# One decode step of attention beside an MLP: the rounds of the loops and the joining of the partial softmaxes rewritten

## Chip, core and metric

The kernel runs on one core of a Trainium2 chip. The metric is the device time of one execution in microseconds. Three runs of the kernel before gave 675.93, 675.94 and 676.19 us; their median is 675.94.

## What is computed

Two tokens (B = 2) go through two branches, which a gate mixes. Branch A is a multi-head attention with a cache: 16 heads of width 256, 4096 cached keys and values per head and token, all float32. Branch B is an MLP with 1792 hidden columns.

```python
g = sigmoid((x * gate_w).sum(-1, keepdims=True))
q = (x @ wq).reshape(B, Sq, H, Dh).transpose(0, 2, 1, 3)      # x: 2 x 1 x 448
scores = einsum("bhqd,bhkd->bhqk", q, k_cache) * Dh ** -0.5
o = einsum("bhqk,bhkd->bhqd", softmax(scores), v_cache)
a = o.transpose(0, 2, 1, 3).reshape(B, Sq, H * Dh) @ wo       # 4096 x 448
b = maximum(einsum("bsd,df->bsf", x, w1), 0) @ w2
return g * a + (1 - g) * b
```

The caches hold 268 MB, which are read once.

## The kernel before

A **unit** is one head of one token; there are U = 32. Its keys and values, 64 KB for each of 128 partitions (8.39 MB), come with one DMA into one of three slots of SBUF. SP issues all large loads, in this order: `wq` into slot 2, units 0 and 1 into slots 0 and 1, the other units in a loop of ten rounds of three (`more`, L126), then `w12` in two halves into slot 2 (`w1`, `w2`) and `wo` into slot 0 in eight pieces (`late`, L135; the limits of the pieces are `CUTS`, in chunks of 448 columns, 32 in all). Ahead of each load SP waits for the slot's own semaphore (`free`), which VectorE raises after the last operation on a unit; the first one TensorE raises, when `wq` has been used.

Per unit, three engines take turns, tied by the semaphores query, score, top, prob and room. ScalarE copies the unit's query out of `qt` (`pick`, L248, one of three buffers), TensorE multiplies it with the keys into the PSUM tile `ps` (`scores`, L234), VectorE takes the negated maximum `nm` of each row, ScalarE the exponential `prob` with its row sums `ls` (`softmax`, L252), and VectorE eight multiplications with the values in place, whose row sums are the partial outputs `ov` (`values`, L259). TensorE may begin the next unit once the first of the eight is done. The keys of a unit are dealt to four groups of 32 partitions, so each unit has four partial softmaxes.

Each of the three engines has a loop of ten rounds with three units written out in a round (L275). Units 30 and 31 stand behind the loop, written out.

**Joining** (`combine`, L285) makes one softmax of the four partial ones, for 16 units at a time: transposes of `nm` and `ls`, a minimum, exponentials, a sum, a reciprocal and the weights `wb` with the gate; a product with the identity that spreads them over the partitions; their product with `ov` (`os`); four products with `sel` that add up the partitions; and copies into `ot`, which is the stationary operand for `wo`. The first half is joined between units 29 and 30. The second half is joined behind the MLP's second layer, and between its steps TensorE multiplies the first eight chunks of `wo`.

The MLP's layers stand behind unit 31 on TensorE: the first waits for `w1`, the second (14 chunks, `acc`) for `w2`.

**The end** (`project`, L364): chunks 0 to 23 of `wo` are added up in `acc` in four column groups. VectorE copies `acc` to SBUF, and TensorE folds the four groups into `z` with `fold`. The last eight chunks (`TAIL`) are multiplied straight into `z`, in four products each. One copy to `res` and a store end the kernel. Float32 products are issued as two instructions each, so a chunk in `acc` is two instructions and a direct chunk is eight.

Of the kernel before, what the change touches and what calls it, by code (L numbers as in the profile page):

```python
# [8 lines left out]
P, HP = 128, 64  # L9
# [58 lines left out]
def gated_mix_decode(nc, xg, kv, wq, w12, wo, out):  # L68
# [15 lines left out]
    UB = U // NB  # L84
# [4 lines left out]
    assert U == LOOPS * SLOTS + 2 and SLOTS == 3  # L89
# [4 lines left out]
    def bank(name, n=CW):  # L94
# [4 lines left out]
    TAIL = 8  # L99
    names = [*ENGINES, "xg", "w2", *(f"wo{k}" for k in CUTS[1:]), "query", "score", "top", "prob", "room",  # L100
             *(f"land{s}" for s in range(SLOTS)), *(f"free{s}" for s in range(SLOTS)), "out"]
    sem = {n: nc.alloc_semaphore(n) for n in names}
    land = [sem[f"land{s}"] for s in range(SLOTS)]
    free = [sem[f"free{s}"] for s in range(SLOTS)]
# [5 lines left out]
    slot = [sbuf(f"slot{s}", P, LEN) for s in range(SLOTS)]  # L110
# [24 lines left out]
    def late(e):  # L135
        take(e, free[2])
        load(2, w12, land[2], 0, NF * D)(e)
        load(2, w12, sem["w2"], NF * D)(e)
        take(e, free[0])
        for lo, hi in zip(CUTS, CUTS[1:]):  # L140
            load(0, wo, sem[f"wo{hi}"], lo * D, hi * D)(e)
        take(e, free[1])
# [21 lines left out]
    xr = sbuf("xr", P, KC, G, B, RB)  # L164
    pr.raw(dve, lambda e: e.wait_ge(sem["xg"], 16))
    for g in range(G):
        pr.op(dve, lambda e, g=g: e.tensor_copy(xr[:, :, g], xg_sb[:, :, :B, None].to_broadcast([P, KC, B, RB])))  # L167
    xu = sbuf("xu", P, KC, UB // B, B)
    have_x = pr.op(dve, lambda e: e.tensor_copy(xu, xg_sb[:, :, None, :B].to_broadcast([P, KC, UB // B, B])))  # L169
# [16 lines left out]

    pr.raw(pe, lambda e: e.wait_ge(sem["xg"], 16))
    for c in range(KC):
        r = rows_of(c)
        t = mm(pw[0][:, :1], xr[r, c].rearrange("p g b r -> p (g b r)"), xg_sb[r, c, B:], c == 0, c == KC - 1, have_x)  # L190
    gp = sbuf("gp", P, 1)
    gate_read = t = activate(gp, pw[0][:, :1], AF.Sigmoid, t)
    omg = sbuf("omg", P, 1)
    have_omg = pr.op(dve, lambda e: e.tensor_scalar(omg, gp, -1.0, 1.0, op0=ALU.mult, op1=ALU.add), t)
    for c in range(KC):
        r = rows_of(c)
        t = mm(pw[1][:UB, :1], xu[r, c].rearrange("p u b -> p (u b)"), xg_sb[r, c, B:], c == 0, c == KC - 1)
    gu = sbuf("gu", UB, 1)
    have_gu = activate(gu, pw[1][:UB, :1], AF.Sigmoid, t)
# [8 lines left out]
    for i in range(NB):  # L208
        w = slot[2][:, i * WQ:(i + 1) * WQ]
        for c in range(KC):  # L210
            for g in range(G):
                r = rows_of(c, g // 2)
                at = g * W + c * CW if c < KF else G * W + g % 2 * CW
                lhs, rhs = flat(xr[r, c, g]), w[r, at:at + CW]
                last = mm(pw[2 + i][g * R:(g + 1) * R, :], lhs, rhs, c == 0, c == KC - 1)
        t = activate(wide, pw[2 + i], AF.Copy, last, *busy[1], scale=SCALE)
        pt = pw[i]
        for k in range(2 * T):
            t2 = transpose(pt[:, k * P:(k + 1) * P], wide[:, k * P:(k + 1) * P], t, gate_read, have_gu)
        busy[1] = (t2,)  # L220
        for s in range(2):
            dst = qt.rearrange("p t (i g s b) -> p i s t g b", i=NB, g=G, s=2)[:, i, s]
            src = pt[:, ::RB].rearrange("p (s t g b) -> p s t g b", s=2, t=T, g=G)[:, s]
            have_q = activate(dst, src, AF.Copy, t2)
# [7 lines left out]
    query = [sbuf(f"query{s}", P, T) for s in range(SLOTS)]  # L232

    def scores(e, u, s):  # L234
        take(e, land[s], 16)
        take(e, sem["query"])
        take(e, sem["room"])
        for c in range(SG // CW):
            for t in range(T):
                for g in range(G):  # L240
                    lo = t * S + g * SG + c * CW
                    m = e.matmul(ps[g * R:(g + 1) * R, c * CW:(c + 1) * CW],  # L242
                                 query[s][:, t:t + 1].to_broadcast([P, R]), slot[s][:, lo:lo + CW],
                                 start=(t == 0), stop=(t == T - 1))
                    if c == SG // CW - 1 and t == T - 1:
                        m.then_inc(sem["score"], 1)

    def pick(e, u, s):  # L248
        e.activation(query[s], qt[:, :, bass.ds(u, 1)].rearrange("p t o -> p (t o)"), AF.Copy).then_inc(  # L249
            sem["query"], 1)  # L250

    def softmax(e, u, s, more=True):  # L252
# [3 lines left out]
        if more:  # L256
            pick(e, u + 1, (s + 1) % SLOTS)

    def values(e, u, s):  # L259
# [3 lines left out]
        for j in range(J):  # L263
            v = slot[s][:, T * S + j * SG:T * S + (j + 1) * SG]
# [3 lines left out]
            if j == J - 1:  # L268
                m.then_inc(free[s], 1)

    stages = {pe: scores, act: softmax, dve: values}
    pr.raw(pe, lambda e: (e.sem_inc(sem["room"], 1), e.drain().then_inc(free[2], 1)))
    pr.raw(act, lambda e: pick(e, 0, 0), have_q)
    for e in stages:
        pr.loop(e, LOOPS, lambda e_, i, e=e: [stages[e](e_, i * SLOTS + s, s) for s in range(SLOTS)])  # L275

    nb, e4, el, lsum, rl = (sbuf(n, UB, k) for n, k in (("nb", 1), ("e4", G), ("el", G), ("lsum", 1), ("rl", 1)))
    wb = sbuf("wb", UB, G, R)  # L280
    os = sbuf("os", P, UB, J)
    ot = sbuf("ot", P, NB, HH, J, B, RB)


    def combine(i, done):  # L285
        us = slice(i * UB, (i + 1) * UB)
        tp, wp, po = pw[0], pw[1], pw[2]
        transpose(tp[:UB, :P], nm[:, us], done)
        t = transpose(tp[:UB, P:2 * P], ls[:, us])
        mt = tp[:UB, 0:P:R]  # L290
        lt = tp[:UB, P:2 * P:R]
        t = pr.op(dve, lambda e: e.tensor_reduce(nb, mt, axis=AX.X, op=ALU.min), t)  # L292
        t = activate(e4, mt, AF.Exp, t, bias=nb, scale=-1.0)
        t = pr.op(dve, lambda e: e.scalar_tensor_tensor(el, e4, 1.0, lt, op0=ALU.mult, op1=ALU.mult, accum_out=lsum),
                  t)
        t = pr.op(dve, lambda e: e.reciprocal(rl, lsum), t)
        t = pr.op(dve, lambda e: e.tensor_scalar(wb, e4[:, :, None].to_broadcast([UB, G, R]), rl, gu, op0=ALU.mult,
                                                 op1=ALU.mult), t, have_gu)
        yield
        t = mm(wp[:, :UB], wb.rearrange("u g r -> u (g r)"), ident[:UB, :UB], True, True, t)  # L300
        t = pr.op(dve, lambda e: e.tensor_tensor(os, ov[:, us], wp[:, :UB, None].to_broadcast([P, UB, J]),
                                                 op=ALU.mult), t)
        yield
        n = HH * B * J
        for q in range(G):
            t2 = mm(po[q * R:(q + 1) * R, :n], sel, os.rearrange("p u j -> p (u j)")[:, q * n:(q + 1) * n], True, True,
                    t)
        for hh in range(HH):
            t = pr.op(dve, lambda e, hh=hh: e.tensor_copy(  # L309
                ot[:, i, hh], po[:, hh * B * J:(hh + 1) * B * J].rearrange("p (b j o) -> p j b o", j=J, o=1)  # L310
                .to_broadcast([P, J, B, RB])), t2)
        have_ot.append(t)

    have_ot = []
    for _ in combine(0, pr.op(dve, lambda e: e.drain())):  # L315
        pass
    for u in range(LOOPS * SLOTS, U):
        for e, f in stages.items():
            more = (u + 1 < U,) if e == act else ()
            pr.raw(e, lambda e_, f=f, u=u, more=more: f(e_, u, u % SLOTS, *more))  # L320
# [9 lines left out]
    for c in range(KC):  # L330
        for g in range(G):
# [3 lines left out]
            t = mm(ph[g * R:(g + 1) * R, :FG], flat(xr[r, c, g]), w1[r, at:at + FG], c == 0, c == KC - 1)  # L335
    t = activate(hs, ph[:, :FG], AF.Relu, t, have_omg, *busy[1], scale=omg)
    for k in range(KF):
        t2 = transpose(pt[:, k * P:(k + 1) * P], hs[:, k * P:(k + 1) * P], t, have_ot[0])
# [9 lines left out]

    pr.raw(pe, lambda e: e.wait_ge(sem["w2"], 16))
    for k in range(NF):  # L350
        g = k % G
        mm(acc[g * R:(g + 1) * R, :], hr[:, k, :], w2[:, k * D:(k + 1) * D], k < G, False, have_hr)
    pr.raw(pe, lambda e: take(e, sem["room"]))
    w = slot[0]

    def lhs(k):
        i, k = divmod(k, HH * J)
        return flat(ot[:, i, k // J, k % J])

# [4 lines left out]
    def project(lo, hi):  # L364
        for k in range(lo, hi):
            if k in CUTS:
                pr.raw(pe, lambda e, s=sem[f"wo{CUTS[CUTS.index(k) + 1]}"]: e.wait_ge(s, 16))
            if k < n:
                g = k % G
                t = mm(acc[g * R:(g + 1) * R, :], lhs(k), w[:, k * D:(k + 1) * D], False, k >= n - G,  # L370
                       have_ot[k // (HH * J)])
            else:
                for g in range(G):
                    t = mm(z[g * R:(g + 1) * R, :DG], lhs(k), w[:, k * D + g * DG:k * D + (g + 1) * DG], False,
                           k == NO - 1)
# [79 lines left out]
```

## Time and profile before

| | |
|---|---|
| median of three runs | 675.94 us |
| profiled execution, its own time | 675.89 us |
| its span (first to last instruction) | 674.6 us |
| busy: VectorE, TensorE, ScalarE | 341.5, 220.4, 59.7 us |
| read from HBM | 289.54 MB, 429 GB/s over the span |

The span is what the trace shows; all times of rows count from its start. Busy times add up the instructions of an engine. TensorE's are modelled and overlap each other, since matmuls are pipelined. For a kernel of this kind the rate of the DMA over the span and what happens after the last landing tell more than the busy shares.

### The profile page before, as it was taken

What the parts mean: (1) busy time and instruction counts of PE and PEld (TensorE: products, weight loads), DVE (VectorE), ACT (ScalarE), POOL (GpSimd) and SP (SyncE); (2) the same over time, 40 slices, a digit from 0 to 9 for tenths busy, and PEclk for the clock granted to TensorE, in tenths of its full rate; (3) what the DMA queues carried; (4) which work ended last, traced back from release to release, by engine and by line L of the source; (5) the groups of instructions that cost most, each with busy time, mean ns of one, the idle gap of its engine ahead of it and who ended that gap; (6) DMA issues with size and microseconds to landing.
All of it is one profiled execution on the core that took longest, in us unless ns stands there. A gap on an engine that the chain in (4) does not pass through costs nothing. (4 is left out here: it accounts for less than half of the span.)

```text
span 674.6 us, 4162 instructions
## 1 busy us (share of the span) xinstructions
PE 220.4 (33%) x1323; PEld 67.6 (10%) x1323; DVE 341.5 (51%) x571; ACT 59.7 (9%) x121; POOL 0.7 (0%) x6
## 2 busy tenths in 40 slices
PE   0653212333332213333321233333223333331367
PEld 0210000001001000100100010010001001000012
DVE  0006565643655665364566636455564643657661
ACT  0010001001000100100010010001001001000010
POOL 0000000000000000000000000000000000000000
PEclk9976566776656677676556667655666766655789
DMA  9999999999999999999999999999999999999997
GB/s 381 428 435 436 436 435 435 435 435 435 435 435 435 435 435 435 435 435 435 431 435 435 435 435 435 435 435 435 435 435 435 431 435 435 435 435 435 403 424 310
DMA packets 6372, 289.61 MB, mean 429 GB/s; under 512 B 864, under 2 KB 1120, under 8 KB 1632
## 3 DMA queue, kind: packets, MB, share of 16 engines
q1 hardware_dynamic: 6224, 289.55, 99.3%
q8 instruction: 3, 0.05, 0.0%
q10 hardware_dynamic: 144, 0.01, 0.0%
q14 instruction: 1, 0.01, 0.0%
HBM read 289.54 MB, written 0.01 MB: 429 GB/s over the span
## 5 line engine op out<-in xcount | busy, mean ns | idle before, releaser
L265 DVE SCALAR_TENSOR_TENSOR slot<-slot,prob 128x1024 f32<-128x1024 f32 x256 | 295.9, 1221 | 65.3 <-DVEq L65 65.3
L242 PE MATMUL ps<-slot,query 128*32 128x512 f32 x1024 | 186.3, 890 | 406.4 <-PEq L65 406.3
L261 DVE TENSOR_REDUCE nm<-ps 128x1024 f32 (+1 forms) x32 | 39.2, 1224 | 228.8 <-DVEq L65 228.8
L242 PEld LDWEIGHTS ps<-slot,query 128*32 128x32 f32 x1024 | 55.7, 156 | 535.5 <-issue 534.9
L254 ACT ACTIVATE prob<-ps,nm 128x1024 f32<-128x1024 f32 x32 | 35.6, 1113 | 367.2 <-ACTq L65 367.1
L254 ACT ACT_TABLE_LOAD x10 | 12.8, 1283 | 178.7 <-ACTq L65 178.7
L265 DVE DVE_READ_ACCUMULATOR slot<-slot,prob (+1 forms) x256 | 21.2, 83 | 0.0
L178 PE MATMUL pw<-slot,xr 128*32 128x512 f32 (+3 forms) x96 | 13.5, 696 | 1.7 <-PEq L65 1.7
L167 DVE COPY xr<-xg_sb 128x128 f32<-128x128 f32 x4 | 0.6, 220 | 18.5 <-DMA xg_sb<-in_xg 18.5
L178 PE MATMUL pw<-xg_sb,xr 128*128 128x1 f32 (+1 forms) x8 | 1.9, 352 | 21.7 <-DVE xu L169 21.7
L178 PE MATMUL acc<-slot,hr 128*32 128x448 f32 x28 | 6.1, 945 | 2.7 <-DMA slot<-in_w 2.7
L249 ACT ACTIVATE query<-qt 128x2 f32 (+1 forms) x32 | 6.2, 193 | 0.0
L254 ACT ACTIVATION_READ_ACCUMULATOR prob<-ps,nm (+1 forms) x32 | 6.2, 193 | 0.0
L178 PE MATMUL acc<-slot,ot 128*32 128x448 f32 x48 | 5.4, 547 | 1.3 <-DMA slot<-in_wo 1.3
L181 PE MATMUL pw<-ident,nm 128*16 128x128 f32 x2 | 0.7, 330 | 12.6 <-DVEq L315 12.6
L178 PEld LDWEIGHTS pw<-slot,xr 128*32 128x32 f32 (+1 forms) x96 | 2.9, 122 | 10.7 <-issue 10.7
L178 PEld LDWEIGHTS pw<-xg_sb,xr 128*128 128x128 f32 (+1 forms) x8 | 1.8, 320 | 21.6 <-DMA xg_sb<-in_xg 21.6
L181 PE MATMUL pw<-ident,wide 128*128 128x128 f32 x11 | 1.9, 288 | 2.4 <-ACT wide L184 2.4
L383 DVE COPY wide<-acc 128x448 f32<-128x448 f32 x1 | 0.6, 625 | 3.9 <-PE acc L178 3.9
L292 DVE TENSOR_REDUCE nb<-pw 16x1 f32<-16x4 f32 x2 | 0.3, 150 | 4.5 <-PE pw L181 4.5
L178 PE MATMUL pw<-slot,ot 128*32 128x112 f32 x64 | 2.3, 265 | 0.3 <-DMA slot<-in_wo 0.2
L309 DVE COPY ot<-pw 128x256 f32<-128x256 f32 x4 | 1.5, 419 | 1.4 <-PE pw L178 1.4
(42 smaller groups left out, 20.3 us busy)
## 6 DMA issues: line engine op xcount, KB each, us to landing
slot<-in_wq SPq DMA_DIRECT2D x1, 7168.0 KB, 19.8
slot<-in_w SPq DMA_DIRECT2D x2, 3136.0 KB, 30.8
slot<-in_wo SPq DMA_DIRECT2D x2, 1792.0 KB, 20.3
slot<-in_wo SPq DMA_DIRECT2D x3, 896.0 KB, 25.6
slot<-in_kv SPq DMA_DIRECT2D x32, 39.0
slot<-in_wo SPq DMA_DIRECT2D x1, 448.0 KB, 27.9
slot<-in_wo SPq DMA_DIRECT2D x2, 224.0 KB, 28.0
xg_sb<-in_xg ACTq DMA_DIRECT2D x1, 6.0 KB, 20.0
```

Source lines behind the costliest of these rows:

```text
L167: pr.op(dve, lambda e, g=g: e.tensor_copy(xr[:, :, g], xg_sb[:, :, :B, None].to_broadcast([P, KC, B, RB])))
L178: return pr.op(pe, lambda e: e.matmul(out, lhs, rhs, start=start, stop=stop), *after)
L181: return pr.op(pe, lambda e: e.transpose(out, src, ident), *after)
L242: m = e.matmul(ps[g * R:(g + 1) * R, c * CW:(c + 1) * CW], query[s][:, t:t + 1].to_broadcast([P, R]), slot[s][:, lo:lo + CW], start=(t == ...
L249: e.activation(query[s], qt[:, :, bass.ds(u, 1)].rearrange("p t o -> p (t o)"), AF.Copy).then_inc(sem["query"], 1)
L254: e.activation(prob, ps, AF.Exp, bias=nm[:, bass.ds(u, 1)], accum_out=ls[:, bass.ds(u, 1)]).then_inc(sem["prob"], 1)
L261: e.tensor_reduce(nm[:, bass.ds(u, 1)], ps, axis=AX.X, op=ALU.max, negate=True).then_inc(sem["top"], 1)
L265: m = e.scalar_tensor_tensor(v, v, 1.0, prob, op0=ALU.mult, op1=ALU.mult, accum_out=ov[:, bass.ds(u, 1), j])
L292: t = pr.op(dve, lambda e: e.tensor_reduce(nb, mt, axis=AX.X, op=ALU.min), t)
L309: t = pr.op(dve, lambda e, hh=hh: e.tensor_copy(ot[:, i, hh], po[:, hh * B * J:(hh + 1) * B * J].rearrange("p (b j o) -> p j b o", j=J, o= ...
L383: t = pr.op(dve, lambda e: e.tensor_copy(a_sb, acc), t)
```

## The change

- TensorE runs eleven rounds of the loop over all units: two units, and behind a condition on the round a third one, which the last round leaves out. ScalarE and VectorE run 32 rounds of one unit each. Nothing is written out behind the loops.
- VectorE finds a unit's slot by arithmetic on a register; the three slots are one tensor. The query has one buffer, which ScalarE writes at the start of a round. The three `free` semaphores are one.
- All 32 units are joined at once. TensorE does the transposes behind the sixth of the 14 chunks of the MLP's second layer, the product with the identity behind the tenth, and the rest behind the fourteenth. No chunk of `wo` is multiplied before `ot` is there.
- `TAIL` is 4 for 8: chunks 24 to 27 go into `acc`.
- The stationary operands made of x hold one copy for a group, not four; a copy on ScalarE (`xw`) makes the wide one for the gate, and the gate for the 16 units of a half is no longer computed by itself.
- On the host, units are ordered by token first, then head.

The core of the diff:

```diff
-    TAIL = 8
+    TAIL = 4
@@ SP
-            take(e, free[s])
+            take(e, sem["free"])
@@ the units
+    def score_rounds(e, i):
+        for s in range(U - LOOPS * SLOTS):
+            scores(e, s)
+        with e.If(i < LOOPS):
+            for s in range(U - LOOPS * SLOTS, SLOTS):
+                scores(e, s)
+
-    def softmax(e, u, s, more=True):
+    def softmax(e, u):
+        e.activation(query, qt[:, :, bass.ds(u, 1)].rearrange("p t o -> p (t o)"), AF.Copy).then_inc(sem["query"], 1)
         take(e, sem["top"])
         e.activation(prob, ps, AF.Exp, bias=nm[:, bass.ds(u, 1)], accum_out=ls[:, bass.ds(u, 1)]).then_inc(
             sem["prob"], 1)
-        if more:
-            pick(e, u + 1, (s + 1) % SLOTS)
-    def values(e, u, s):
+    def values(e, u):
+        at = e.snap(u % SLOTS * LEN)
...
-            v = slot[s][:, T * S + j * SG:T * S + (j + 1) * SG]
+            v = slots[:, bass.ds(at + (T * S + j * SG), SG)]
...
+    pr.loop(pe, LOOPS + 1, score_rounds)
+    pr.loop(act, U, softmax)
+    pr.loop(dve, U, values)
@@ behind the loops
-    for _ in combine(0, pr.op(dve, lambda e: e.drain())):
-        pass
-    for u in range(LOOPS * SLOTS, U):
-        ...
+    second(0, NF - 8)
+    transpose(tp[:U, :P], nm, done)
+    t = transpose(tp[:U, P:2 * P], ls)
+    second(NF - 8, NF - 4)
...
+    t1 = mm(wp[:, :U], wb.rearrange("u g r -> u (g r)"), ident[:U, :U], True, True, t)
+    second(NF - 4, NF)
...
+    for q in range(G):
+        t2 = mm(po[q * R:(q + 1) * R, :NB * cols], sel, os[:, :, q].rearrange("p i h j b -> p i (h j b)"), True, True, t)
+    for i in range(NB):
+        have_ot.append(pr.op(dve, lambda e, i=i: e.tensor_copy(
...
-    at = 0
-    for _ in combine(1, done):
-        project(at, at + NO // 8)
-        at += NO // 8
-    t = project(at, n)
+    t = project(0, n)
```

## Rows read from the trace of the kernel before

**Rows 1.** The page's DMA rate in GB/s, in 40 equal slices of 16.9 us.
```profile
GB/s 381 428 435 436 436 435 435 435 435 435 435 435 435 435 435 435 435 435 435 431 435 435 435 435 435 435 435 435 435 435 435 431 435 435 435 435 435 403 424 310
```

**Rows 2.** The chain of waits that ended last, its end: start, length (us), what.
```profile
643.93 27.99 DMA slot<-in_wo
...
671.96 0.52 PE pw L178 x8
...
672.51 0.28 DVE res L388
```

**Rows 3.** The timeline, units 1 and 27: start, length (us), engine, line, operation [idle before <-releaser].
```profile
59.81 5.35 PE L242 MATMUL ps<-slot,query 128*32 128x512 f32 x32 [12.94 <-PEq L65]
...
562.59 6.61 PE L242 MATMUL ps<-slot,query 128*32 128x512 f32 x32 [13.36 <-PEq L65]
...
570.91 1.28 ACT L254 ACT_TABLE_LOAD   x1 [18.59 <-ACTq L65]
572.20 1.11 ACT L254 ACTIVATE prob<-ps,nm 128x1024 f32<-128x1024 f32 x1
```

**Rows 4.** The timeline, units 30 and 31 and the MLP.
```profile
628.66 1.23 DVE L261 TENSOR_REDUCE nm<-ps 128x1 f32<-128x1024 f32 x1 [4.75 <-DVEq L65]
...
639.87 5.45 PE L242 MATMUL ps<-slot,query 128*32 128x512 f32 x32 [11.46 <-PEq L65]
...
647.03 3.35 PE L178 MATMUL pw<-slot,xr 128*32 128x448 f32 x32 [1.71 <-PEq L65]
...
654.84 6.06 PE L178 MATMUL acc<-slot,hr 128*32 128x448 f32 x28 [2.71 <-DMA slot<-in_w]
...
656.30 1.22 DVE L265 SCALAR_TENSOR_TENSOR slot<-slot,prob 128x1024 f32<-128x1024 f32 x1
```

**Rows 5.** Sequencer instructions of single lines: count, shortest/median/longest ns, first to last start.
```profile
L46 PEldq COMPARE_BRANCH  x10: 76/208/217, 81.6 to 603.1; - x10
...
L254 ACT ACT_TABLE_LOAD  x10: 1283/1283/1283, 48.7 to 570.9; - x10
...
L265 DVEq FUSED_REGOPS  x240: 57/57/57, 51.3 to 611.7; - x120
```

**Rows 6.** The timeline, the joining of the first half.
```profile
620.00 0.42 PE L181 MATMUL pw<-ident,ls 128*16 128x128 f32 x1
...
621.70 0.60 PE L178 MATMUL pw<-ident,wb 16*128 16x16 f32 x2 [1.27 <-DVE wb L297]
622.34 0.29 DVE L301 TENSOR_TENSOR os<-ov,pw 128x128 f32<-128x128 f32 x1 [0.70 <-PE pw L178]
...
622.68 0.34 PE L178 MATMUL pw<-os,sel 128*32 128x32 f32 x8 [0.38 <-DVE os L301]
...
623.16 0.76 DVE L309 COPY ot<-pw 128x256 f32<-128x256 f32 x2 [0.54 <-PE pw L178]
```

**Rows 7.** The timeline, `wo` and the fold.
```profile
663.65 1.69 PE L178 MATMUL acc<-slot,ot 128*32 128x448 f32 x16
...
667.63 0.96 PE L178 MATMUL acc<-slot,ot 128*32 128x448 f32 x8 [1.17 <-DMA slot<-in_wo]
668.73 0.62 DVE L383 COPY wide<-acc 128x448 f32<-128x448 f32 x1 [3.89 <-PE acc L178]
...
669.41 0.40 PE L178 MATMUL pw<-wide,fold 128*32 128x112 f32 x8 [0.82 <-DVE wide L383]
669.78 0.73 PEld L178 LDWEIGHTS pw<-slot,ot 128*32 128x32 f32 x32 [0.22 <-DMA slot<-in_wo]
669.78 2.02 PE L178 MATMUL pw<-slot,ot 128*32 128x112 f32 x56
```

**Rows 8.** Busy time of each engine by stretch, then TensorE's granted clock, DMA share, GB/s.
```profile
660.00:662.00 2.00, 2.00 (x14) 0.26 (x10) 0.39 (x4) 0.25 (x1) 0.00 (x0) 0.84 0.95 405
```

**Rows 9.** The page: the queue for code (packets, MB, share), and `xg` (us to landing).
```profile
q8 instruction: 3, 0.05, 0.0%
...
xg_sb<-in_xg ACTq DMA_DIRECT2D x1, 6.0 KB, 20.0
```

More of the change, by code (lines that the diff above doesn't have):

```diff
@@ L88, in gated_mix_decode @@
     LOOPS = (U - 2) // SLOTS
-    assert U == LOOPS * SLOTS + 2 and SLOTS == 3
+    assert U == LOOPS * SLOTS + 2 and SLOTS == 3 and U == R
     def sbuf(name, *shape):
@@ L98, in gated_mix_decode @@
     CUTS = (0, NO // 4, NO // 2, NO - 12, NO - 8, NO - 4, NO - 2, NO - 1, NO)
-    TAIL = 8
-    names = [*ENGINES, "xg", "w2", *(f"wo{k}" for k in CUTS[1:]), "query", "score", "top", "prob", "room",
-             *(f"land{s}" for s in range(SLOTS)), *(f"free{s}" for s in range(SLOTS)), "out"]
+    TAIL = 4
+    names = [*ENGINES, "xg", "w2", *(f"wo{k}" for k in CUTS[1:]), "query", "score", "top", "prob", "room", "free",
+             *(f"land{s}" for s in range(SLOTS)), "out"]
     sem = {n: nc.alloc_semaphore(n) for n in names}
     land = [sem[f"land{s}"] for s in range(SLOTS)]
-    free = [sem[f"free{s}"] for s in range(SLOTS)]
     pr = Program(nc)
@@ L109, in gated_mix_decode @@
     sbuf("gap", P, -(-(-nc.sbuf_base // 32) * 32) % 1024 // 4)
-    slot = [sbuf(f"slot{s}", P, LEN) for s in range(SLOTS)]
+    slots = sbuf("slots", P, SLOTS * LEN)
+    slot = [slots[:, s * LEN:(s + 1) * LEN] for s in range(SLOTS)]
     ps = bank("ps", SG)
@@ L135, in late @@
     def late(e):
-        take(e, free[2])
+        take(e, sem["free"])
         load(2, w12, land[2], 0, NF * D)(e)
         load(2, w12, sem["w2"], NF * D)(e)
-        take(e, free[0])
+        take(e, sem["free"])
         for lo, hi in zip(CUTS, CUTS[1:]):
             load(0, wo, sem[f"wo{hi}"], lo * D, hi * D)(e)
-        take(e, free[1])
+        take(e, sem["free"])
     pr.raw(sp, late)
@@ L161, in gated_mix_decode @@
                                                      op0=ALU.mult), t)
-    xr = sbuf("xr", P, KC, G, B, RB)
+    xr = sbuf("xr", P, KC, B, RB)
     pr.raw(dve, lambda e: e.wait_ge(sem["xg"], 16))
[L166 to L169, printed above, removed]
+    have_x = pr.op(dve, lambda e: e.tensor_copy(xr, xg_sb[:, :, :B, None].to_broadcast([P, KC, B, RB])))
     def rows_of(c, i=0):
@@ L189, in gated_mix_decode @@
         r = rows_of(c)
-        t = mm(pw[0][:, :1], xr[r, c].rearrange("p g b r -> p (g b r)"), xg_sb[r, c, B:], c == 0, c == KC - 1, have_x)
+        t = mm(pw[0][:, :1], xw[r, c].rearrange("p g r -> p (g r)"), xg_sb[r, c, B:], c == 0, c == KC - 1, have_xw)
     gp = sbuf("gp", P, 1)
-    gate_read = t = activate(gp, pw[0][:, :1], AF.Sigmoid, t)
+    have_gp = gate_read = t = activate(gp, pw[0][:, :1], AF.Sigmoid, t)
     omg = sbuf("omg", P, 1)
     have_omg = pr.op(dve, lambda e: e.tensor_scalar(omg, gp, -1.0, 1.0, op0=ALU.mult, op1=ALU.add), t)
[L195 to L199, printed above, removed]
     qt = sbuf("qt", P, T, U)
@@ L218, in gated_mix_decode @@
         for k in range(2 * T):
-            t2 = transpose(pt[:, k * P:(k + 1) * P], wide[:, k * P:(k + 1) * P], t, gate_read, have_gu)
+            t2 = transpose(pt[:, k * P:(k + 1) * P], wide[:, k * P:(k + 1) * P], t, gate_read)
         busy[1] = (t2,)
         for s in range(2):
-            dst = qt.rearrange("p t (i g s b) -> p i s t g b", i=NB, g=G, s=2)[:, i, s]
+            dst = qt.rearrange("p t (b i g s) -> p i s t g b", i=NB, g=G, s=2)[:, i, s]
             src = pt[:, ::RB].rearrange("p (s t g b) -> p s t g b", s=2, t=T, g=G)[:, s]
@@ L231, in gated_mix_decode, with scores @@
     prob = sbuf("prob", P, SG)
-    query = [sbuf(f"query{s}", P, T) for s in range(SLOTS)]
-    def scores(e, u, s):
+    query = sbuf("query", P, T)
+    def scores(e, s):
         take(e, land[s], 16)
@@ L242, in scores @@
                     m = e.matmul(ps[g * R:(g + 1) * R, c * CW:(c + 1) * CW],
-                                 query[s][:, t:t + 1].to_broadcast([P, R]), slot[s][:, lo:lo + CW],
+                                 query[:, t:t + 1].to_broadcast([P, R]), slot[s][:, lo:lo + CW],
                                  start=(t == 0), stop=(t == T - 1))
@@ L268, in values @@
             if j == J - 1:
[L269 to L312, printed above, removed]
@@ L314, in gated_mix_decode @@
-    have_ot = []
-    for _ in combine(0, pr.op(dve, lambda e: e.drain())):
-        pass
-    for u in range(LOOPS * SLOTS, U):
-        for e, f in stages.items():
-            more = (u + 1 < U,) if e == act else ()
-            pr.raw(e, lambda e_, f=f, u=u, more=more: f(e_, u, u % SLOTS, *more))
+                m.then_inc(sem["free"], 1)
+    pr.raw(pe, lambda e: (e.sem_inc(sem["room"], 1), e.drain().then_inc(sem["free"], 1)))
+    pr.raw(act, lambda e: None, have_q)
+    pr.loop(pe, LOOPS + 1, score_rounds)
@@ L345, in gated_mix_decode, with second @@
                            pt[r, KF * P + j * HP:KF * P + (j + 1) * HP].rearrange("p (k r) -> p k r", r=R), AF.Copy)
+    def second(lo, hi):
+        for k in range(lo, hi):
+            g = k % G
+            mm(acc[g * R:(g + 1) * R, :], hr[:, k, :], w2[:, k * D:(k + 1) * D], k < G, False, have_hr)
     pr.raw(pe, lambda e: e.wait_ge(sem["w2"], 16))
-    for k in range(NF):
-        g = k % G
-        mm(acc[g * R:(g + 1) * R, :], hr[:, k, :], w2[:, k * D:(k + 1) * D], k < G, False, have_hr)
+    second(0, NF - 8)
@@ new lines, in gated_mix_decode @@
+    nb, e4, el, lsum, rl = (sbuf(n, U, k) for n, k in (("nb", 1), ("e4", G), ("el", G), ("lsum", 1), ("rl", 1)))
+    wb = sbuf("wb", U, G, R)
+    os = sbuf("os", P, NB, G, HH, J, B)
+    ot = sbuf("ot", P, NO, B, RB)
+    tp, wp, po = pw[0], pw[1], pw[3]
+    transpose(tp[:U, :P], nm, done)
+    t = transpose(tp[:U, P:2 * P], ls)
+    second(NF - 8, NF - 4)
+    mt = tp[:U, 0:P:R]
+    lt = tp[:U, P:2 * P:R]
+    t = pr.op(dve, lambda e: e.tensor_reduce(nb, mt, axis=AX.X, op=ALU.min), t)
+    t = activate(e4, mt, AF.Exp, t, bias=nb, scale=-1.0)
@@ L369, in project @@
                 g = k % G
[L370 removed]
+                t = mm(acc[g * R:(g + 1) * R, :], flat(ot[:, k]), w[:, k * D:(k + 1) * D], False, k >= n - G,
                        have_ot[k // (HH * J)])
@@ L427 @@
     order = np.arange(H).reshape(NB, HH, G).transpose(0, 2, 1).reshape(H)
-    kt = np.asarray(A_k_cache).reshape(B, H, S, T, P).transpose(1, 0, 4, 3, 2)[order].reshape(U, P, T * S)
-    vt = np.asarray(A_v_cache).reshape(B, H, G, SG, R, J).transpose(1, 0, 2, 4, 5, 3)[order].reshape(U, P, J * SG)
+    kt = np.asarray(A_k_cache).reshape(B, H, S, T, P)[:, order].transpose(0, 1, 4, 3, 2).reshape(U, P, T * S)
+    vt = np.asarray(A_v_cache).reshape(B, H, G, SG, R, J)[:, order].transpose(0, 1, 2, 4, 5, 3).reshape(U, P, J * SG)
     kv = np.concatenate([kt, vt], 2)
```

32 lines of the change are left out of this document (20 added, 12 removed).

## The prediction

> **What bounds the kernel now.** I read the slices of DMA traffic first: from the second slice on the core moves 428 to 436 GB/s in all but one slice until the last two, although no compute engine is near full [rows 1]. The reader is to see a kernel that is one long transfer, with all arithmetic beside it. The chain of waits, read second, says the same of the end: the last piece of `wo` was issued at 643.93 us and waited 27.99 us in the queue behind other data; it landed at 671.92, and only the last chunk's eight matmuls, one copy and the store followed [rows 2]. So the end is "last landing of `wo`" plus 0.52 us of TensorE, 0.28 us of VectorE and the store. The same bytes go through the same queue in the same order after the change, so a new time can come from three places alone: a hole in the queue, a longer tail behind the last landing, or arithmetic that is no longer done when `wo` has landed.
>
> The profiled execution took 675.89 us with a span of 674.60, so 1.29 us lie outside the span; the median of the three runs is 675.94. I make the sum in the span and carry 1.29 + 0.05 us over.
>
> **The rounds.** Every unit's scores start when its data lands: unit 1's at 59.81, unit 31's at 639.87, so 19.34 us for each of the 30 units between, which at 8.39 MB is 434 GB/s; ten rounds of the loop lie in it, so the branch back costs the stream nothing [rows 3, 4]. VectorE's wait ahead of a unit's first reduction is 4.75 us in a late, short case [rows 4], and it is longer in the others. Three things are added per unit.
>
> First, branches: the loop's own costs 0.208 us on TensorE (median), the dearest of all engines [rows 5]. One per unit instead of one per three on VectorE, and a second one per round on TensorE (the condition), lie in these waits: nothing.
>
> Second, address arithmetic: 0.057 us for one register operation ahead of a VectorE instruction [rows 5]. The remainder, the slot's address and two addresses for each of eight multiplications are perhaps 20 of these, 1.2 us per unit. The multiplications take 1.22 us each [rows 4], so theirs lie under work that is queued; the first one's, some 0.3 us, don't. To be felt, they would have to fill the 4.75 us.
>
> Third, table loads: ten in the loop's ten rounds of three [rows 5], ahead of the round's first ScalarE activation, which is the exponential: 1.28 us, and the exponential starts at 572.20 instead of 570.91 [rows 3]. The two units behind it in the round have none. After the change there are 32 rounds, so I expect 32 loads; the round's first activation is now the copy of the query, and there the load is done while ScalarE waits: cost nothing. If it stays with the exponential, every unit gets 1.28 us later, units 30 and 31 too, which have no load now. I take nothing, since the load stands ahead of the first activation in all ten rounds, and keep 1.28 for the range. (The Trainium skill, ScalarE: Activation LUTs, section "What ACT_TABLE_LOAD costs", gives about 2.66 us for each switch, with a drain. The rows show 1.29 us between the load's start and the exponential's, so the trace doesn't agree here; by the page the bound would be 1.4 us wider.)
>
> The single query buffer is written after the exponential of the unit before it, so after TensorE has read the old one; it is ready over 10 us before its data. The one semaphore for free slots counts up in the order in which the slots are taken. Neither adds a wait on SP: SP issues a load one unit and more ahead of its turn: the last piece of `wo` at 643.93, while the second half of `w12` lands only at 654.84 [rows 2, 4].
>
> **The head.** One copy instead of five on VectorE and a new 128x512 copy on ScalarE of about 0.6 us, then no second gate product: the query work shifts by some tenths and has until 40 us, when unit 0 lands. Nothing.
>
> **The joining.** Now half of it is done before unit 30, with `wo`'s first half multiplied beside the second half's joining. After the change TensorE reaches unit 30 without it, some 2 to 3 us earlier (the steps from the transposes to the `ot` copies took from 620 to 623.9 [rows 6]), so `wo` is issued earlier, with the queue full anyway: no gain. Unit 31 is bound by its landing as now (scores at 639.87) and VectorE's last multiplication ended at 657.52 [rows 4]; with the 0.3 us from above, 657.85. Then, at half clock where the rows are:
> - Second layer up to there: it starts at 654.84 with the landing of `w2`; 12 of 28 instructions at 6.06/28 = 0.216 us, done at 657.4 [rows 4].
> - Two transposes, 0.6 us (the second alone took 0.42 and ended at 620.42): 658.45. VectorE's and ScalarE's small steps up to `wb`: 1.25 us (620.42 to the product at 621.70): 659.7; eight second-layer instructions beside them: 658.45 + 1.7 = 660.15 [rows 6].
> - The product with the identity 0.6 us: 660.75; `os` twice as wide, 0.29 + 128 columns at about 1 ns = 0.42: 661.2; the last eight second-layer instructions to 662.45; the eight selecting products some 0.5: 662.95; the first `ot` copy, 512 columns for 256 of 0.38 us, 0.7 us: 663.7 [rows 6].
> - 24 chunks of `wo`, 48 instructions at 1.69/16 = 0.106 us: 5.1 us, done at 668.8. The next chunks land at 669.78 [rows 7]. TensorE has caught up with 1.0 us to spare.
>
> So the joining, though over 10 us later for half of the chunks, is hidden by the landing of `wo`. Its cover is this 1.0 us.
>
> **Four direct chunks for eight.** This is the one term on the end. Chunks 24 to 27 now go through the accumulator, so the copy of it and the fold stand behind the landing at 669.78, not behind the one at 667.63. Eight instructions 0.96 us: 670.74; copy 0.14 later and 0.62 long: 671.50; fold from 671.57 [rows 7]. By then nearly all of `wo` is there (671.92 the last [rows 2]). Behind the fold's start stand 8 + 32 small products. The 56 of before took 2.02 us with their waits, 0.036 us each [rows 7]. Their weight loads bound them from below, 32 in 0.73 us. So 40 take 1.0 to 1.45 us; I take 1.2, near the lower, since the 56 were held up by landings: 672.77, result copy 0.15 behind: 672.92 for 672.51 now. That is +0.4 us (0.2 to 0.65), and the rest of the tail is unchanged.
>
> Sum: 674.6 + 0.4 = 675.0 in the span, 676.3 in the time. Bounds: -0.3 with the runs' own spread and the smallest tail, and upward: with 1.28 us on unit 31 the 24 chunks end at 670.1, 0.3 us late; with a clock that rises 2 us late another 0.5 to 1.
>
> **Rivals.**
> *TensorE stays at half clock* (slower). The granted clock was 0.84 on the mean of 660 to 662, so it rose to the upper level (2.4 GHz) in there [rows 8], with TensorE working from 654.84 on; unit 27's scores ran all 6.61 us at the half clock [rows 3]. The new order waits about half a us ahead of the transposes and one ahead of the `wo` products. At half clock the 48 instructions need 10.4 us and the next 8 1.7: 675.8; copy and fold 0.83, 40 products 2.1: 678.8, +6.3 us: 682.2. It decides from a rise later than about 667. Against it: apart from these gaps TensorE works without pause from 654.84 on, so a rise by 665 is likely.
>
> *Code behind a branch must be fetched* (slower). Behind the loop stands all of the MLP, now at once after unit 31, where two unrolled units stood. A fetch that queued beside the stream like the 6 KB of `xg`, 20.0 us to landing [rows 9], would start the MLP at 665.3 instead of 647.03 (its cover is the wait of 1.7 us there and 2.7 for `w2` [rows 4]), so behind all landings: 5.1 us to the second layer (7.8 less that 2.7), 8.9 to the first `ot`, 5.9 of `wo`, 2.2 to the result: 687.4 for 672.51, +14.9 us: 690.8. Against it: the code queue moved 3 packets in all [rows 9], and behind the loop's exit now the joining's second transpose ran at 620.00, about when unit 30 landed (639.87 less 19.34) [rows 4, 6]. The Trainium skill (Runtime: NRT & Kernel Launch, section "Instruction fetch mechanics") states that a taken branch out of the window that is held forces such a fetch; the ten taken branches of TensorE here, 0.208 us, show none [rows 5].
>
> *A hole in the queue closes* (faster). The slice from 624 to 641 moved 403 GB/s, 1.25 us short of 435, and the next 424, 0.4 us [rows 1]. If that were SP's late issue of `wo`, the earlier issue would give it back: 676.3 - 1.65 = 674.6. Against it: `w12` was in flight until 654.84.
>
> **How the numbers follow.** Forecast 0.84 (675.5 to 677.3); half clock, in full or in part, 0.07; code fetch 0.04; earlier stream 0.04; the rest, a VectorE round beyond 19.3 us, 0.01. A measurement tells about 0.2% from no change, 1.35 us: 674.6 to 677.3. The forecast lies within but for its upper edge (0.02); the first, second and last cases lie above, the third about the lower bound. Faster 0.03, within 0.83, slower 0.14. Range 675.5 to 677.6.
>
> **What would show it.** Landing of the last `wo` piece at 672 as now; one TensorE group of 40 small products that starts near 671.6 and doesn't wait; 32 table loads, ahead of the query's copy; the first `ot` near 663.7 and a wait for `wo` ahead of chunk 24. Wrong: a landing that moved, no wait for `wo` behind 664, a half clock past 667, or an idle TensorE behind unit 31.

## The result, and the profile after

The changed kernel takes 676.74 us (median of 22 executions, 676.15 to 678.54) for 676.15 of the kernel before beside it (22 executions, 675.59 to 676.72): a ratio of 1.0013, 95% interval 1.0007 to 1.0019. It is slower by 0.6 us, within the 0.2% that the prediction counted as no change; 676.3 was forecast, with a range of 675.5 to 677.6. The median hides that the executions spread: 16 of the 22 lie between 676.15 and 677.13, six between 677.48 and 678.54. No execution of the kernel before lay above 676.72. The profiled execution is the slowest of all, 678.54 us with a span of 676.9, so what follows first is one of the six. One disturbed execution each of e6 and e9 below (698.22 and 750.84 us) is left out.

The page of the changed kernel, its groups (operation, count | busy, mean ns | idle before), shows the table loads:

```profile
L252 ACT ACTIVATE prob<-ps,nm 128x1024 f32<-128x1024 f32 x32 | 35.7, 1114 | 529.1 <-ACTq L65 529.1
L250 ACT ACT_TABLE_LOAD x32 | 41.1, 1283 | 0.7 <-ACT qt L180 0.2
L250 ACT ACTIVATE query<-qt 128x2 f32 x32 | 6.5, 204 | 0.4
```

32 loads for the ten of [rows 5], all at the line of the query's copy. The timeline (start, length) of one unit shows where they lie, the second fence unit 31 and the joining:

```profile
104.98 1.23 DVE L258 TENSOR_REDUCE nm<-ps 128x1024 f32 x1 [5.90 <-DVEq L65]
106.41 1.11 ACT L252 ACTIVATE prob<-ps,nm 128x1024 f32<-128x1024 f32 x1 [15.47 <-ACTq L65]
107.63 1.28 ACT L250 ACT_TABLE_LOAD   x1
```

```profile
640.42 6.19 PE L236 MATMUL ps<-slots,query 128*32 128x512 f32 x32 [13.71 <-PEq L65]
...
647.59 3.35 PE L174 MATMUL pw<-slots,xr 128*32 128x448 f32 x32 [0.98 <-PEq L65]
...
650.00 1.23 DVE L262 SCALAR_TENSOR_TENSOR slots<-slots,prob 128x1024 f32 x1 [1.82 <-DVEq L65]
...
658.02 1.22 DVE L262 SCALAR_TENSOR_TENSOR slots<-slots,prob 128x1024 f32 x1
...
659.35 0.39 PE L177 MATMUL pw<-ident,nm 128*32 128x128 f32 x1 [1.05 <-DVEq L273]
...
664.20 1.29 DVE L336 COPY ot<-pw 128x512 f32<-128x512 f32 x2 [1.56 <-PE pw L174]
665.03 7.65 PE L174 MATMUL acc<-slots,ot 128*32 128x448 f32 x56 [0.99 <-DVE ot L336]
```

The exponential starts 0.2 us behind the maximum, with no load between, and the load runs behind it, while VectorE multiplies. At the end, the 56 products with `wo` run in one piece, without the wait for chunk 24 that was forecast: TensorE has not caught up with the landings. The chain of waits that ended last no longer goes through `wo`'s DMA [rows 2] but through TensorE:

```profile
665.03 7.77 PE acc L174 x56
...
672.83 0.64 DVE wide L364
...
673.51 1.29 PE pw L174 x40
...
674.82 0.28 DVE res L369
```

The stretches (length, busy time of each engine, then TensorE's granted clock, DMA share, GB/s) say why in the main:

```profile
656.00:658.00 2.00, 2.00 (x12) 0.22 (x4) 2.00 (x3) 0.00 (x0) 0.00 (x0) 0.50 1.01 430
...
666.00:668.00 2.00, 2.00 (x14) 0.45 (x9) 0.00 (x0) 0.00 (x0) 0.00 (x0) 0.50 1.01 423
668.00:670.00 2.00, 2.00 (x20) 0.71 (x16) 0.00 (x0) 0.00 (x0) 0.00 (x0) 0.63 0.99 398
670.00:672.00 2.00, 2.00 (x28) 0.68 (x22) 0.00 (x0) 0.00 (x0) 0.00 (x0) 1.00 0.40 152
```

TensorE stayed at the lower level (1.2 GHz) up to about 669.5. Before, it had risen between 660 and 662 [rows 8]. In this execution the half-clock rival came true in part; in most others it can't have, by their times. The stream was late here too: unit 31's scores start at 640.42 for 639.87, and the last piece of `wo`, issued at 642.7, landed 29.8 us later, at 672.5 for 671.92 [rows 2].

### The profile page after: what moved, and what is told of

Read it like the earlier page. It is cut to its first block, busy times and chain, and to the rows that moved or that the text cites. A ratio compares the mean times of both kernels' runs of the same rounds, so it can differ in the third digit from the quotient of the medians.

```text
span 676.9 us, 4262 instructions
## 1 busy us (share of the span) xinstructions
PE 221.2 (33%) x1279; PEld 58.5 (9%) x1279; DVE 339.8 (50%) x559; ACT 93.0 (14%) x143; POOL 0.7 (0%) x6
## 5 line engine op out<-in xcount | busy, mean ns | idle before, releaser
L236 PE MATMUL ps<-slots,query 128*32 128x512 f32 x1024 | 188.0, 901 | 425.7 <-PEq L65 425.7
L262 DVE SCALAR_TENSOR_TENSOR slots<-slots,prob 128x1024 f32 x256 | 295.9, 1221 | 58.2 <-DVEq L65 58.2
L258 DVE TENSOR_REDUCE nm<-ps 128x1024 f32 x32 | 39.2, 1225 | 250.3 <-DVEq L65 250.3
L236 PEld LDWEIGHTS ps<-slots,query 128*32 128x32 f32 x1024 | 47.1, 157 | 566.0 <-issue 566.0
L262 DVE DVE_READ_ACCUMULATOR slots<-slots,prob x256 | 21.2, 83 | 0.0
L174 PE MATMUL pw<-slots,xr 128*32 128x512 f32 (+3 forms) x96 | 12.7, 661 | 6.6 <-PEq L65 6.6
L174 PE MATMUL acc<-slots,ot 128*32 128x448 f32 x56 | 7.7, 712 | 1.0 <-DVE ot L336 1.0
L174 PE MATMUL acc<-slots,hr 128*32 128x448 f32 x28 | 6.3, 906 | 2.8 <-DMA slots<-in_w 2.8
L250 ACT ACTIVATE query<-qt 128x2 f32 x32 | 6.5, 204 | 0.4
L252 ACT ACTIVATION_READ_ACCUMULATOR prob<-ps,nm x32 | 6.2, 193 | 0.0
## 6 DMA issues: line engine op xcount, KB each, us to landing
slots<-in_wo SPq DMA_DIRECT2D x2, 224.0 KB, 29.8
```

What stands on the lines that cost most here:

```text
L174: return pr.op(pe, lambda e: e.matmul(out, lhs, rhs, start=start, stop=stop), *after)
L236: m = e.matmul(ps[g * R:(g + 1) * R, c * CW:(c + 1) * CW], query[:, t:t + 1].to_broadcast([P, R]), slot[s][:, lo:lo + CW], start=(t == 0), ...
L250: e.activation(query, qt[:, :, bass.ds(u, 1)].rearrange("p t o -> p (t o)"), AF.Copy).then_inc(sem["query"], 1)
L252: e.activation(prob, ps, AF.Exp, bias=nm[:, bass.ds(u, 1)], accum_out=ls[:, bass.ds(u, 1)]).then_inc(sem["prob"], 1)
L258: e.tensor_reduce(nm[:, bass.ds(u, 1)], ps, axis=AX.X, op=ALU.max, negate=True).then_inc(sem["top"], 1)
L262: m = e.scalar_tensor_tensor(v, v, 1.0, prob, op0=ALU.mult, op1=ALU.mult, accum_out=ov[:, bass.ds(u, 1), j])
```

## Experiments

Each kernel ran beside the kernel before on the same chip. Three groups, with 676.11 (e1 to e4), 676.07 (e5 to e8) and 676.32 us (e9 to e11) as the median of the kernel before. "Upper" executions are those more than 1 us above it; the kernel before had 1 of 33, 0 of 29 and 4 of 28 of them. The first group ran on one chip, the other two on another.

| run | what | median, us | over before | upper |
|---|---|---|---|---|
| e1 | the changed kernel | 677.16 | +1.05 | 6 of 11 |
| e2 | changed, eight direct chunks | 676.34 | +0.23 | 2 of 11 |
| e3 | before, four direct chunks | 676.69 | +0.58 | 5 of 11 |
| e4 | changed, six early extra products | 676.86 | +0.75 | 4 of 11 |
| e5 | e4 with eight direct chunks | 676.53 | +0.46 | 1 of 11 |
| e6 | e4 and three late extra products | 676.77 | +0.70 | 1 of 11 |
| e7 | e3 and the three late ones | 676.33 | +0.26 | 0 of 11 |
| e8 | changed, table load on the exponential | 678.47 | +2.40 | 5 of 5 |
| e9 | e6, table load on the exponential | 677.16 | +0.84 | 4 of 11 |
| e10 | e6, joining 2.3 us later | 678.13 | +1.81 | 12 of 12 |
| e11 | changed, late extra products alone | 677.73 | +1.41 | 8 of 12 |

### e1: the changed kernel again

No edit.

> The changed kernel itself, to see an execution other than the profiled one, in which TensorE stayed at half clock until about 669 us. My theory (two cases): most executions take 0.2 to 0.7 us more than before, since the four direct chunks and the fold stand behind a later landing; some take 1 to 2.5 us more, those in which the clock rises only while wo is being multiplied. Median +0.4 to +0.8 us. If this trace has an early rise, its wo products start near 664 and then wait for wo ahead of chunk 24. Rival (the joining is simply too late, whatever the clock): no such wait in any trace, and no cluster of runs near +0.4.

The lower half of the executions lies at +0.3 to +1.0, the rest up to +2.9; the median is above what I expected. The trace that came is again one of a late rise (678.99 us, clock 0.50 from 658 to 668), so it shows no wait either. The clean case had to come from e2 and e4.

```profile
668.00:670.00 2.00, 2.00 (x16) 0.48 (x11) 0.00 (x0) 0.00 (x0) 0.00 (x0) 0.51 0.99 395
670.00:672.00 2.00, 2.00 (x28) 0.77 (x24) 0.00 (x0) 0.00 (x0) 0.00 (x0) 1.00 0.34 131
```

### e2: eight direct chunks

```diff
-    TAIL = 4
+    TAIL = 8
```

> The changed kernel with eight direct chunks again. My theory: the lower cluster of runs comes back to that of the kernel before (0.0 to +0.2 us, so 0.3 to 0.6 less than the changed kernel), because the copy and the fold stand behind the landing of chunk 23 again; the upper runs (half clock) stay. Rival (four direct chunks cost nothing, the joining costs it all): no difference from the changed kernel within 0.2 us.

Nine of eleven lie between 676.00 and 676.56. That is my theory's price of the four direct chunks given back, and two upper executions stay (678.14 and 678.56). This trace has an early rise. The products of `wo`, and one stretch:

```profile
662.55 3.96 PE L174 MATMUL acc<-slots,ot 128*32 128x448 f32 x40 [1.04 <-DVE ot L336]
667.66 0.96 PE L174 MATMUL acc<-slots,ot 128*32 128x448 f32 x8 [1.14 <-DMA slots<-in_wo]
```

```profile
658.00:660.00 2.00, 1.40 (x12) 0.27 (x10) 1.08 (x7) 0.25 (x1) 0.00 (x0) 1.00 1.04 444
```

With the clock up by 658, 20 chunks are done by 666.5 and TensorE waits 1.14 us for the next ones: the joining is hidden. Up to this point the program is that of the profiled changed kernel, whose clock rose 11 us later. What made the difference isn't shown.

### e3: the kernel before with four direct chunks

```diff
-    TAIL = 8
+    TAIL = 4
```

> The kernel before with four direct chunks for eight and nothing else. My theory: +0.4 us (0.2 to 0.65), without runs above +1, since the first 16 chunks are multiplied ahead of the second half's joining. Rival: within 0.15 us of the kernel before.

The median is at the upper part of what I expected, but five of eleven are upper executions, of which I had expected none: here the joining is early. The trace is of the slowest (678.35 us). Its chain, and its last stretches:

```profile
670.21 1.84 PE acc L178 x8
...
672.08 0.64 DVE wide L383
...
672.75 2.22 PE pw L178 x40
```

```profile
666.00:668.00 2.00, 0.88 (x8) 0.07 (x8) 0.00 (x0) 0.00 (x0) 0.00 (x0) 1.00 0.99 414
668.00:670.00 2.00, 0.96 (x8) 0.16 (x8) 0.00 (x0) 0.00 (x0) 0.00 (x0) 0.94 1.01 406
670.00:672.00 2.00, 1.72 (x8) 0.20 (x8) 0.00 (x0) 0.00 (x0) 0.00 (x0) 0.50 0.31 119
```

The clock was up and **fell** just ahead of 670: from 666 on TensorE had worked 0.9 of each 2 us, between landings. That alone doesn't tell when it falls: in the traces of the kernel before and of e2 TensorE worked 0.83 and 0.86 us from 666 to 668, and the clock stayed at 1.00. Then the eight products behind the landing of chunk 24 took 1.84 us, where they take 1.08 at the upper level (e4), and the 40 small ones 2.22 for 1.29. That is +1.7 us in this trace, on the path only because of the four direct chunks. With eight, little more than the last eight small products stands behind a landing.

### e4: six extra products early

Products into an unused bank, meant for where TensorE waits anyway; `spin(n)` is n products of `ident` with a 512-wide tile.

```diff
+    spin(3)
     pr.raw(pe, lambda e: e.wait_ge(sem["w2"], 16))
     second(0, NF - 8)
+    spin(3)
```

> The changed kernel with six extra products of the identity with a 512-wide tile into an unused PSUM bank, three ahead of TensorE's wait for w2 and three ahead of its wait for the last unit's values; they keep TensorE at work where it waits. They add work and take none away. My theory (the clock makes the upper runs): the runs above +1 us vanish, the median falls to +0.3 to +0.5, the trace shows full clock over 656 to 672 and a wait for wo ahead of chunk 24. Rival (the joining is too late whatever the clock): the spread stays, the median is the same or up to 0.5 higher.

The trace does what I expected, the times only in part: the median is +0.75, and four of eleven stay upper, but at +1.2 to +1.6 now, not up to +2.9. The clock is at 1.00 from 644 to 674. The second three products last longer than the wait they fill: VectorE's last multiplication ends at 658.20, the transposes start at 659.37, behind them.

```profile
663.47 3.96 PE L175 MATMUL acc<-slots,ot 128*32 128x448 f32 x40 [1.04 <-DVE ot L343]
667.79 0.96 PE L175 MATMUL acc<-slots,ot 128*32 128x448 f32 x8 [0.35 <-DMA slots<-in_wo]
669.95 0.96 PE L175 MATMUL acc<-slots,ot 128*32 128x448 f32 x8 [1.20 <-DMA slots<-in_wo]
671.05 0.62 DVE L371 COPY wide<-acc 128x448 f32<-128x448 f32 x1 [7.13 <-PE acc L175]
671.73 0.40 PE L175 MATMUL pw<-wide,fold 128*32 128x112 f32 x8 [0.82 <-DVE wide L371]
...
673.04 0.28 DVE L376 COPY res<-pw 128x112 f32<-128x112 f32 x1 [1.37 <-PE pw L175]
```

This is the end as forecast, step by step: the wait ahead of chunk 24 (1.20 us), then 3.09 us from its landing to the result's copy, where the prediction had 669.78 to 672.92, 3.14 us. Together with e3 it left two half-clock stretches, a late rise at the joining and a fall behind 666, and one rival: that the stream's landings make the rest.

### e5: six early products and eight direct chunks

Edits of e2 and e4.

> The changed kernel with eight direct chunks and with the six extra products ahead of the second layer and of the joining. Two theories of the runs above +1 us are left. Mine: there are two half-clock stretches, a late rise at the joining (cured by the extra products) and a fall behind 666 us between the landings of wo, which costs much only with four direct chunks, since eight accumulated products, the copy and 40 small products then run behind the last long wait. Then this kernel has no runs above +1 us, median 0.0 to +0.2 over the kernel before. Rival (late landings of the stream make the upper runs): upper runs stay, at +1 to +1.7.

Ten of eleven lie within +0.7, so the upper ones are gone but for one (679.70, at a mean granted clock of 0.60 over its span, which the others don't have; no trace of it). The median is +0.46 for 0.0 to +0.2: a miss, with an interval of the ratio from 1.0000 to 1.0019. In its trace the last landing's products start at 672.48 for 671.96 [rows 2], with unit 31 at 640.28 for 639.87, so here the stream itself came 0.4 to 0.5 us late. Over the traces of this study unit 31 starts between 639.86 and 641.03, with the earliest and the latest of them on kernels that differ by the tail alone (e2, e1): the landings of this unit spread by about 1 us between executions, those of the last piece of `wo` by 0.8 (671.9 in e8 to 672.7 in e1). By my estimate a median of eleven isn't good for less than some 0.3.

### e6 and e7: three late extra products

One of 256 columns ahead of the wait for chunks 20 to 23, one of 512 ahead of 24 to 27, one of 256 during the copy. In e6 beside the six early ones, in e7 alone, on e3's kernel.

```diff
+            if k in (20, 24):
+                spin(1, 256 if k == 20 else 512)
...
     t = pr.op(dve, lambda e: e.tensor_copy(a_sb, acc), t)
+    spin(1, 256)
```

> The changed kernel (four direct chunks) with the six extra products and three more in the waits behind them: one of 256 columns ahead of the wait for chunks 20 to 23, one of 512 ahead of the wait for chunks 24 to 27, one of 256 during the copy ahead of the fold. My theory: no runs above +1 us any more, median +0.3 to +0.6 over the kernel before: the four direct chunks' own price. Rival (the stream's landings): runs at +1 to +1.7 as without the three.

> The kernel before with four direct chunks and with the same three late extra products, none earlier. My theory: the upper runs that this kernel had without them (5 of 11 above +1 us) vanish, median +0.3 to +0.5 over the kernel before. Rival: they stay.

Work was added, and the upper executions went but for one: in e7 none of 11, for 5 in e3, and the highest is 676.78; in e6 one of 11, at +1.16. These are small counts, and e3 ran on the other chip. In e7's trace the clock is 1.00 from 662 on, and the chain is again the landing of chunk 24 and 3.1 us:

```profile
669.90 0.96 PE L179 MATMUL acc<-slot,ot 128*32 128x448 f32 x8
670.79 0.70 PE L179 MATMUL junk<-xr,ident 128*128 128x256 f32 x2
...
673.00 0.28 DVE L396 COPY res<-pw 128x112 f32<-128x112 f32 x1 [1.37 <-PE pw L179]
```

So the four direct chunks cost +0.26 (e7) at a clock that is held, a little below what I had expected there; with an interval of the ratio from 0.9995 to 1.0013 the times alone don't exclude nothing. e6's +0.70 is above +0.6, and its trace (the +1.16, with the clock at 1.00 from 646 on) says that it isn't the price of the four chunks alone. The chain that ended last goes through no landing of `wo`; it is TensorE's own work, the extra products (`junk`) included:

```profile
664.02 3.97 PE acc L175 x40
667.98 0.63 PE junk L175 x2
668.61 0.89 PE acc L175 x8
669.50 1.06 PE junk L175 x2
670.56 1.01 PE acc L175 x8
...
673.58 0.28 DVE res L379
```

### e8 and e9: the table load on the exponential

The query's copy goes behind the exponential, so that the exponential is the first activation of a round; a first copy ahead of the loop and one more column of `qt` go with it (not shown below). In e9 with the nine extra products.

```diff
-        e.activation(query, qt[:, :, bass.ds(u, 1)]...).then_inc(sem["query"], 1)
         take(e, sem["top"])
         e.activation(prob, ps, AF.Exp, ...)
+        e.activation(query, qt[:, :, bass.ds(u + 1, 1)]...).then_inc(sem["query"], 1)
```

> The changed kernel with ScalarE's query copy moved behind the exponential, so that the exponential is the round's first activation. My theory: the 32 table loads move to the exponential, each unit's first multiplication starts 1.28 us later after its maximum, and the time rises by 0 to 0.4 us where the clock is up early (the cover of the joining is 1.0 us), by 1.3 in runs in which wo's products end the chain; median 0.2 to 1.0 above the changed kernel. Rival (the load is on no path wherever it stands): no change.

The load moved as expected (unit 31):

```profile
647.90 1.28 ACT L253 ACT_TABLE_LOAD   x1 [15.99 <-ACTq L65]
649.20 1.11 ACT L253 ACTIVATE prob<-ps,nm 128x1024 f32<-128x1024 f32 x1
```

The time rose more than my theory had: 1.3 us above e1, 2.4 above the kernel before, in all five. Either the 1.28 us pass through, and the cover of 1.0 us isn't there, or they lower the clock again, since TensorE waits that much longer ahead of the joining. The trace can't say: in it the granted clock never got above 0.75 behind 28 us, with a mean of 0.591 over the span, where the other four executions have 0.655 to 0.671. e9 was to tell them apart.

> The kernel with all nine extra products (six early, three late), and with the table loads on the exponential as in the run that rose to 2.4 us over the kernel before. Theory A (the clock made that rise, since TensorE then waits 1.28 us longer ahead of the joining): with the clock held up the load costs 0 to 0.4 us, median +0.6 to +1.0 over the kernel before. Theory B (1.28 us of delay simply pass through, the cover isn't there): +1.7 to +2.0.

Median +0.84, in the range of theory A; of that 0.70 is there without the load (e6). The two come from different groups, so 0.1 us is not more than "little", and seven of eleven lie at +0.2 to +1.0. Four lie above, three of them at 680.4 to 680.7. The trace is of a lower one, with the clock at 1.00 from 644 on; what made those four stays open.

But e9 doesn't decide between the theories. In its trace the chain runs through the extra products ahead of the transposes (657.20 to 659.97), as in e6 (657.30 to 660.08), so VectorE and the load ahead of it are not on the chain at all. The extra products both hold the clock up and give VectorE slack, so whether the 1.28 us pass through in e8 or act by the clock is not shown.

### e10: the joining 2.3 us later

Two multiplications on VectorE behind the last unit, 1.15 us apart, on e6.

> The kernel with all nine extra products, and two more multiplications of 1024 columns on VectorE behind the last unit, so that the joining starts 2.3 us later. With a cover of 1.0 to 1.3 us, as the prediction had it and as the trace with the six early products has it, 1.0 to 1.3 us come through, less what the late products overlap: median +1.4 to +2.0 over the kernel before. If the cover is nil: +2.9 to +3.1. If it is over 2.3: +0.6 to +0.7.

+1.81, which is 1.1 more than e6, as forecast for a cover of 1.0 to 1.3 us; two of the twelve lie at +5.0 and +5.4, of which there is no trace. The traces, with the clock at 1.00, don't bear that cover out:

```profile
665.54 3.97 PE acc L175 x40
...
675.11 0.28 DVE res L383
```

From e6 to e10 the `wo` products start 1.52 us later and the result's copy 1.53 later: nothing is covered behind the joining, since e6's late extra products had filled the waits already. Most of what is missing of the 2.3 us went ahead of the joining, where e6's transposes (659.91) were waiting for the early extra products, VectorE having been done at 659.35. So e10 is no measure of the changed kernel's cover.

### e11: the late products alone

The three late products of e6, without the six early ones.

> The changed kernel with the three late extra products alone. Theory of two half-clock stretches: the late rise at the joining stays, so runs at +1 to +2.5 us stay (a third or more of them), and where TensorE is late the extra products add up to 1 us, since they stand in its way: median +0.7 to +1.6. If the late fall were all, no upper runs and +0.3 to +0.7.

Eight of twelve are upper, so the late rise is there without any late fall:

```profile
665.22 6.09 PE L175 MATMUL acc<-slots,ot 128*32 128x448 f32 x40 [1.00 <-DVE ot L341]
```

20 chunks took 6.09 us, for 3.96 in e2 and e4; the clock was 0.50 from 656 to 668 and 0.61 over 668 to 670. The trace is of the slowest (+4.17). With TensorE that late the extra products stand in its way: from the first `wo` product to the copy of `acc` it takes 9.69 us (665.22 to 674.91), for 7.80 in the changed kernel (665.03 to 672.83), so 1.9 us for the 1 at most that I expected.

## Why the prediction was right, and where it was not

**Rounds.** Right. Branches now cost 0.208 us on TensorE (11) and 0.056 on VectorE (32) and lie in waits. The table loads went to the copy of the query, as the place ahead of the first activation had it. (The prediction called 4.75 us a short wait of VectorE's; the shortest in that trace is 4.71.) The first multiplication starts 0.51 us behind the exponential's end (648.38 + 1.11 to 650.00), where unit 27 had 0.33 and unit 31 0.24: +0.27 for the 0.3 that were taken.

**Code behind the branch.** Right to leave it at 0.04: the MLP starts at 647.59, 7.2 us behind unit 31's landing, as before (647.03 behind 639.87 [rows 4]).

**The joining.** Its steps were right, and with the clock up it is covered: in e4 TensorE waits 1.20 us ahead of chunk 24, for the 1.0 forecast, and 0.35 ahead of chunk 20, although the extra products hold the transposes up there; in e2 it waits 1.14 us ahead of chunk 20. The sum had the joining at the lower level and `wo` at the upper, a start of `wo` at 663.7; the traces show either an earlier one (662.55 in e2) or a later one (665.03 in the changed kernel, with unit 31 0.55 late), and in the latter no cover.

**Four direct chunks.** Right in mechanism and about in size: 3.09 us behind the landing of chunk 24 for 3.14 in the sum; in the time +0.26 (e7), +0.41 (the 16 lower executions of the changed kernel, median 676.56 for 676.15) and +0.7 (the five lower ones of e1 less the nine of e2) for +0.4. Counted from the last landing, which takes the spread of the landings out, the result's copy starts 0.6 us behind it in the kernel before (671.92 to 672.51) 0.9 in e4 (672.1 to 673.04) and 1.0 in e7 (672.0 to 673.00): +0.3 to +0.4. The 40 small products took 1.29 for 1.2.

**The half clock.** Here the step failed. The prediction gave 0.07, on the ground that "apart from these gaps TensorE works without pause from 654.84 on, so a rise by 665 is likely". The gaps were the point: 1.05 us ahead of the transposes, 1 us ahead of the `wo` products. In the four traces of this order of work without the early extra products the clock fell between 654 and 656 and rose at 658 (e2), 669.5 (after, e11) and 670 (e1); in the five with them (e4, e5, e6, e9, e10) it was at 1.00 from 646 to 672. Of the prediction's own signs of being wrong, the profiled execution shows three: a landing that moved (by 0.6 us), no wait behind 664, and a half clock past 667.

The decision point (a rise later than about 667) and the direction were as the rival had them; its price of +6.3 us was for a clock that never rises. The two traces of the changed kernel lie at +2.4 and +2.9, and not all of that is the clock: the last landing is 0.6 and 0.75 us later than before, and the four direct chunks cost 0.4. That leaves, by estimate, 1.4 and 1.7 us for a rise at 669.5 and 670.

In the changed kernel 12 of 33 executions lie more than 1 us above the kernel before, and both traces of it are of such ones. That all twelve had a late rise is not shown: e6's trace lies at +1.16 with the clock up.

**What was not seen at all** is the fall behind 666 us. It takes no change to the joining (e3), and it makes the four direct chunks dearer: +1.7 us in that trace, the only one that shows it. There, the work behind the landing of chunk 24 ran at the level that TensorE had fallen to while it waited.

The median came out right because most executions of the changed kernel are, by their times, free of both: the lower 16 have +0.41 as their median, the forecast's +0.4, and the six upper ones lift the median of all to +0.6. How large the share of upper executions would be, nothing in the sum fixes, so that is luck: had they been over half (677.48 to 678.54), the median would have lain at the range's upper edge of 677.6 or beyond.

No kernel here beats the kernel before, which ends with the landing of `wo`.

## What to carry to other kernels

In a kernel that one transfer bounds, work may be gathered behind the transfer only as far as its cover goes **at the lower clock**, if TensorE waits ahead of it; here a cover of 1 us at the upper level was none at the lower. What must run behind the last landings should be short, and it is safer to price it at half clock too when TensorE has been waiting between landings (e3). Extra products that hold the clock are work as well: once they fill the waits, the chain runs through them (e6, e9, e10), and what the waits had covered can't be read there any more. Where a program's executions spread, one trace is one of several cases: look at the spread of the times before reading it as the kernel's.

## What the runs showed of the hardware

- The same order of work met a rise of TensorE's clock at 658 in one execution (e2) and at 669.5 to 670 in others (after, e1): over 11 us apart.
- The clock fell with no wait longer than 1.21 us, while TensorE worked 0.88 and 0.96 of 2 us (e3); with extra products of 0.7 to 1.1 us in those waits it stayed up in the trace of e7, and without them in those of e2 and e4.
- In one execution (e8) the granted clock stood at 0.75, between the two levels, as its upper value from 28 us to the end (0.75 over 646 to 654 and from 666 on); 56 products took 7.06 us. The execution of e5 at 679.70 has about the same mean over its span (0.60, for 0.591), so it may have been another.

```profile
670.00:672.00 2.00, 2.00 (x20) 0.42 (x12) 0.00 (x0) 0.00 (x0) 0.00 (x0) 0.75 0.10 38
```

- The table load stood ahead of the first activation of every round, whichever that was: the copy (after, 32 times 1.28 us, while ScalarE had nothing else to do) or the exponential (e8). Nothing more than the 1.28 us showed: in the profiled round above it starts at 107.63 and the copy at 108.92.
